# Reordering operand sums, stores and last transposes in an attention and mixture-of-experts kernel with nested Strassen products

## Chip, cores and metric

One core of one Trainium2 chip. The metric is device time in microseconds (us) of one execution; a kernel's figure is the median of its executions. "Span" is the length of the one execution that the profiler took; it is about 1.8 us shorter than the time of the same execution. "Half clock" is a stretch in which the trace shows TensorE's granted clock at one half; the "mean clock" of an execution is that clock's average over it, and 1.000 is full.

## The reference

Linear attention with decay over 4 batches, 8 heads, 768 positions and 64 channels, in blocks of 64, then a four-expert feed-forward on the 3072 x 512 result. All is fp32.

```python
# attention, per block b of 64 positions
intra = ((qb @ kb.T) * Dmask) @ vb
out   = intra + (qb * lam_pow) @ kv_state
kv_state = lam_block * kv_state + (kb * rev_pow).T @ vb
# bridge: x = out as (3072, 512)
p = domain_probs / (domain_probs.sum(-1, keepdims=True) + 1e-09)
for e in range(4):                       # w1: 512 x 1024, w2: 1024 x 512
    h = np.maximum(x @ w1[e], 0.0)
    out += p[:, e:e + 1] * (h @ w2[e])
```

## The kernel before

The expert layers are three groups of 1024 tokens times four experts: twelve **units**. Each x @ w1 of a unit is done by two levels of a seven-product scheme (products M1 to M7, each made of seven inner products), so most matmuls take *sums* of blocks as operands. VectorE and GpSimd make those sums; VectorE also takes the products out of PSUM ("evacuation", `m<-pg`, `m<-pM`) and adds them up (`hS`). Unit one runs beside the attention. From unit two on, TensorE interleaves the second layer of a unit with the first layer of the next. In the last group the second layer is nested too, and its sums (`T1` to `T4`, tiles `hT`) are made on the way.

Python decides the order at build time with lists of closures: `chores` is GpSimd's work and its loads, handed out by `pump` as time slots `now[0]` go by; `queue` holds stores; `background` and `aside` are put-off VectorE and GpSimd steps that `rest()` and `take()` draw from between products. The places that matter here:

```python
def own_x(m):                             # unit two's x operands, (...) is a cut
    ...
            for n, x, y, op in T_OPS:     # four 128x256 subtractions, tile "ops"
                b[n] = s[:, SLOT[n]]
                tt(nc.vector, b[n], b[x], b[y], op)
    ...
def own_w1(m):                            # unit two's w1 operands
    ...
        tt(nc.gpsimd, b[n], b[x], b[y], op)
    ...
def own(m):
    fed[0, 1, m] = own_x(m), own_w1(m)

# the list of GpSimd's work while unit one's last direct products run
chores.extend((*prepare_w2(1), *raws, pause(4), mine["M1"], sum_own("S1", "A21", "A22", ALU.add)))

# last group: operand sums on VectorE, block by block
for at in BLOCKS:
    for n in names:                       # ("T1", "T3", "T2") or ("T4",)
        ...                               # ScalarE copies one block to PSUM, VectorE subtracts
        work.append([lambda n=n, at=at: total(n, at)])
```

## Time and profile before

| kernel before | value |
|---|---|
| time, median of 3 | 1205.98 us (1205.05 to 1207.86) |
| span profiled | 1202.6 us |
| TensorE busy | 1188.0 us, 99% |
| waits of TensorE for unit two's first operands, then for the last unit, then at the end, by spacing | 3.03; 2.02 + 1.23 + 0.72; 0.77 + 0.77 us |
| half clock after the first of these | 3.413 us long, 1.76 us lost |

"By spacing" means: the distance between the starts of two matmul records, less the 0.216 us that a 128x256 record takes when nothing is in the way (0.109 us for the 128x128 transposes at the end). It counts a little more than the idle time that the profile prints. With TensorE at 99%, only such places can be won; the prediction below shows the lines.

```profile
90.50 3.45 POOL L95 TENSOR_TENSOR w1o<-w1o,w1b 128x512 f32<-128x512 f32 x2
103.94 1.41 POOL L95 TENSOR_TENSOR ops<-w1o 128x256 f32<-128x256 f32 x2 [10.00 <-PE pg L733]
```

### The profile page before, as it was taken

How to read it: one execution, taken by the hardware profiler on the slowest of the kernel's cores; microseconds unless marked ns; L12 is line 12 of the kernel's file. 1: busy time of each engine (PE TensorE's matmuls, PEld its weight loads, DVE VectorE, ACT ScalarE, POOL GpSimd, SP SyncE). 2: the span in 40 equal slices, each digit the busy share in tenths (PEclk: the TensorE clock that was granted, in tenths of full speed). 3: DMA queues.
4: the chain of work that ended last, by engine and by line, in shares of the span. 5: the costliest groups of instructions: out<-in, count | busy, mean ns of one | idle time of the engine just before them, and what ended most of it. 6: DMA issues, size and time to landing. Idle time of an engine off the chain costs nothing.

```text
span 1202.6 us, 17908 instructions
## 1 busy us (share of the span) xinstructions
PE 1188.0 (99%) x6623; PEld 1031.2 (86%) x6623; DVE 793.2 (66%) x1318; ACT 261.9 (22%) x476; POOL 635.3 (53%) x600
## 2 busy tenths in 40 slices
PE   9999999999999999999999999999999999999988
PEld 8887888888888888888888888888888888888877
DVE  6597796477467656746755774764665667777774
ACT  3321122112112201311220120120133341241232
POOL 1874267355468800044425745416675774874873
PEclk9999999999999999999999999999999999999999
DMA  9874869999989985789987999898987566566542
GB/s 224 231 262 166 276 208 352 352 315 332 377 286 328 339 286 173 224 286 275 283 286 233 304 311 319 278 315 304 301 280 262 215 229 248 218 241 227 208 151 71
DMA packets 227447, 317.94 MB, mean 264 GB/s; under 512 B 91648, under 2 KB 168864, under 8 KB 227360
## 3 DMA queue, kind: packets, MB, share of 16 engines
q1 hardware_dynamic: 219920, 314.63, 77.6%
q10 hardware_dynamic: 7440, 2.17, 0.8%
q8 instruction: 52, 0.85, 0.3%
q14 instruction: 35, 0.29, 0.1%
HBM read 231.40 MB, written 85.34 MB: 263 GB/s over the span
## 4 chain that ended last, share of the span: by engine, by line
PE 90%; DVE 3%; SPq 3%; DMA 2%; POOL 1%; issue 1%; ACT 0%; DVEq 0%; POOLq 0%
PE pg L733 38%; PE q L787 33%; PE pq L958 12%; DVE m L95 2%; SPq L122 2%; PE sp L484 1%; PE op L512 1%; POOL w2o L95 1%; PE op L507 1%; PE qp L461 1%; PE kp L461 1%; PE pM L928 1%; DMA probs<-in_moe_domain_probs_dram 1%; DMA w1b<-in_moe_w_dram 1%; PE op L520 1%
## 5 line engine op out<-in xcount | busy, mean ns | idle before, releaser
L733 PE MATMUL pg<-xs_in,ws_in 128*128 128x256 f32 x1960 | 470.3, 380 | 0.7 <-DVE m L95 0.5
L733 PEld LDWEIGHTS pg<-xs_in,ws_in 128*128 128x128 f32 x1960 | 370.5, 190 | 53.9 <-DVE m L95 2.5
L95 DVE TENSOR_TENSOR m<-pg,m 128x512 f32<-128x512 f32 x451 | 307.7, 687 | 111.7 <-PE pg L733 101.5
L787 PE MATMUL q<-w2t,hS 128*128 128x256 f32 x1024 | 243.3, 380 | 0.0
L787 PEld LDWEIGHTS q<-w2t,hS 128*128 128x128 f32 x1024 | 192.9, 190 | 26.8 <-issue 0.3
L803 DVE SCALAR_TENSOR_TENSOR acc<-q,gate,acc 128x256 f32<-128x256 f32 x192 | 92.4, 481 | 174.0 <-PE q L787 173.1
L787 PE MATMUL q<-w2t,m 128*128 128x256 f32 x768 | 183.9, 383 | 0.0
L787 PEld LDWEIGHTS q<-w2t,m 128*128 128x128 f32 x768 | 145.9, 191 | 20.6 <-issue 0.2
L745 ACT ACTIVATE m<-m 128x512 f32<-128x512 f32 x132 | 83.0, 630 | 337.1 <-DVE m L95 335.3
L95 POOL TENSOR_TENSOR m<-m,xT 128x512 f32<-128x512 f32 x64 | 81.6, 1290 | 78.4 <-ACT m L745 46.3
L95 POOL TENSOR_TENSOR kn<-kn,s_decay 128x512 f32<-128x512 f32 x20 | 22.1, 1105 | 170.4 <-PE kp L461 130.3
L95 DVE TENSOR_TENSOR sums<-pq,sums 128x256 f32<-128x256 f32 x154 | 64.1, 421 | 49.3 <-PE pq L958 41.7
L958 PE MATMUL pq<-acc,w2t 128*128 128x256 f32 x352 | 86.7, 379 | 1.9 <-POOL acc L95 1.9
L741 ACT COPY m<-pg 128x512 f32<-128x512 f32 x88 | 51.4, 585 | 154.6 <-PE pg L733 147.9
L95 DVE TENSOR_TENSOR m<-m,m 128x512 f32<-128x512 f32 x96 | 81.0, 847 | 0.0
L95 POOL TENSOR_TENSOR ops<-w2b 128x256 f32<-128x256 f32 x24 | 18.9, 807 | 109.6 <-DMA w2b<-in_moe_w_dram 109.6
L958 PEld LDWEIGHTS pq<-acc,w2t 128*128 128x128 f32 x352 | 66.8, 190 | 11.3 <-issue 2.2
L680 ACT ACTIVATE m<-m 128x512 f32<-128x512 f32 x48 | 30.3, 631 | 154.0 <-DVE m L95 154.0
L95 DVE TENSOR_TENSOR hS<-m,m 128x512 f32<-128x512 f32 x64 | 54.8, 861 | 8.4 <-ACT m L745 8.4
L95 POOL TENSOR_TENSOR acc<-hT,hT 128x512 f32<-128x512 f32 x32 | 40.1, 1270 | 32.5 <-DVE hT L95 19.5
L95 POOL TENSOR_TENSOR w2o<-w2b 128x512 f32<-128x512 f32 x32 | 41.8, 1326 | 24.2 <-DMA w2b<-in_moe_w_dram 21.4
L95 POOL TENSOR_TENSOR acc<-hT,acc 128x512 f32<-128x512 f32 x32 | 40.7, 1271 | 5.0 <-PE pq L958 2.7
(129 smaller groups left out, 1325.5 us busy)
## 6 DMA issues: line engine op xcount, KB each, us to landing
xs_in<-x_ops SPq DMA_DIRECT2D x70, 896.0 KB, 6.0
ws_in<-w_ops SPq DMA_DIRECT2D x70, 896.0 KB, 8.6
w2t<-w_ops SPq DMA_DIRECT2D x66, 256.0 KB, 6.6
w2t<-w_sums SPq DMA_DIRECT2D x64, 256.0 KB, 3.8
w_ops<-ops SPq DMA_DIRECT2D x28, 512.0 KB, 5.4
w2t<-in_moe_w_dram SPq DMA_DIRECT2D x48, 256.0 KB, 3.3
x_ops<-ops SPq DMA_DIRECT2D x17, 512.0 KB, 6.8
w2b<-in_moe_w_dram SPq DMA_DIRECT2D x32, 256.0 KB, 5.7
```

Source lines behind the costliest of these rows:

```text
L95: eng.tensor_tensor(out=o, in0=a, in1=b, op=op)
L122: nc.sync.dma_start(out=to[:, :, r], in_=of[:, :, r])
L461: nc.tensor.transpose(out=x[:, ac * C:(ac + 1) * C], in_=y[:, 2 * ac:2 * ac + 2].rearrange("p r d -> p (r d)"), identity=ident[:],)
L484: nc.tensor.matmul(out=sp[r][:, ac * C:(ac + 1) * C], lhsT=hc(kT)[half[r], ac], rhs=hc(qT)[half[r], ac], start=True, stop=True,)
L507: nc.tensor.matmul(out=op[r][half[x], a * C:(a + 1) * C], lhsT=kv[half[r], 2 * a + x], rhs=hc(qs)[half[r], 2 * a + x], start=(a == 0), sto ...
L680: nc.scalar.activation(out=o[:], in_=o[:], func=AF.Relu)
L733: nc.tensor.matmul(out=p[:, j * 256:(j + 1) * 256], lhsT=ws[i][:, j * P:(j + 1) * P], rhs=xs[i], start=(fresh and j == 0), stop=True, skip ...
L741: nc.scalar.copy(out=new[at][:], in_=p[:])
L745: nc.scalar.activation(out=new[at][:], in_=new[at][:], func=AF.Relu)
L787: nc.tensor.matmul(out=p[:, s * DH:(s + 1) * DH], lhsT=h[A_OF[m]][:, c * 256 + s * P:c * 256 + (s + 1) * P], rhs=fed2[g, e, m][uu][:, c], ...
L803: nc.vector.scalar_tensor_tensor(out=o, in0=x, scalar=w, in1=o, op0=ALU.mult, op1=ALU.add)
L958: nc.tensor.matmul(out=p[:, 0:256], lhsT=fed3[e, m, x // 2][:, x % 2, c * P:(c + 1) * P], rhs=b[B_OF[i]][:, c * 256:(c + 1) * 256], start= ...
```

## The change

Its intent is to take away TensorE's remaining waits: (1) at the start, half of the first q and k loads are issued from another engine; (2) for unit two, the w1 operands of the first product are made ahead of w2's sums, and its x operands come earlier in VectorE's order; the stores of x operands wait eight slots in a queue of their own, `late`; (3) for the last unit, VectorE makes T1's four sums first, a put-off step is skipped at the unit's first slot, and M3's GpSimd sums are made in the unit before; (4) at the end, the last blocks are transposed and stored in pieces. Cut to its core:

```diff
-                    nc.sync.dma_start(out=to[:, :, r], in_=of[:, :, r])
+                    by = nc.scalar if n < 2 and r == 1 else nc.sync
+                    by.dma_start(out=to[:, :, r], in_=of[:, :, r])
 (...)
+        while late and (force or late[0][0] <= now[0]):
+            late.pop(0)[1]()
 (...)
-        for at in BLOCKS:
-            for n in names:
+        for part in names:
+            for at in BLOCKS:
+                for n in part:
 (...)   # names: (("T1",), ("T3", "T2")), (("T4",),)
-        keep_own(("x", 0, m), x_ops[0, MS.index(m)], pieces)
+        late.append((now[0] + 8, keep_own(("x", 0, m), x_ops[0, MS.index(m)], pieces)))
 (...)
-    chores.extend((*prepare_w2(1), *raws, pause(4), mine["M1"], sum_own("S1", "A21", "A22", ALU.add)))
+    w2_steps = prepare_w2(1)
+    chores.extend((
+        lambda: own_weights("M1"), sum_own("S1", "A21", "A22", ALU.add), *w2_steps[0:4], mine["M1"], *w2_steps[4:],
+        raw["A12"],
+    ))
 (...)
-                inner_sums(ahead[1], SEQ3[0])
+                inner_sums(ahead[1], SEQ3[0], nested)
+                if ahead[1] == EARLY[0]:
+                    inner_sums(*EARLY, True)
 (...)
-                elif ahead or x % 2 == 0:
+                elif ahead or x % 2 == 0 and x + i:
                     rest()
 (...)
-    give("M4", 1, ("s1",))
+    give("M4", 0, ("q01",), (0,))
+    give("M4", 1, ("q11",), (0,))
```

Cut: small tiles in place of stage tiles for two w1 blocks, a faster pace of handing out GpSimd's work, early operand steps put first in line in `chores`, the order of some loads, and, with the new order of the T sums, an earlier release: the first five of them are put off by four slots in place of six.

More of the change, by code (lines that the diff above doesn't have):

```diff
@@ L121, in load @@
                 for r in range(2):
-                    nc.sync.dma_start(out=to[:, :, r], in_=of[:, :, r])
+                    by = nc.scalar if n < 2 and r == 1 else nc.sync
+                    by.dma_start(out=to[:, :, r], in_=of[:, :, r])
             nat[n, name] = x[:].rearrange("p (h d) -> p h d", d=D)
-    lam_bc = consts.tile([P, H], FP32, name="lam_bc")
-    nc.scalar.dma_start(out=lam_bc[:], in_=lam.partition_broadcast(P))
     w1_ops = dram.tile([E, 7, P, 7, 256], FP32, name="w1_ops")
@@ L135 @@
     X_AT = {n: i for i, n in enumerate(("M1", "M7", "M6", "M4", "M5", "M2", "M3"))}
-    chores, queue, results, made = [], [], [], set()
+    chores, queue, late, results, made = [], [], [], [], set()
     LEFT = 1
@@ L333, in raw_w1 @@
         i, j = int(name[1]) - 1, int(name[2]) - 1
-        if name == "A22":
+        if name in ("A21", "A22"):
             to = tuple(small("w1b")[:] for _ in range(2))
@@ L344, in sum_w1 @@
     def sum_w1(e, name, a, b, op):
-        if e == 0:
+        if e == 0 or name == "S1":
             to = tuple(small("w1o")[:] for _ in range(2))
@@ L352, in sum_w1 @@
         w1_now[e][name] = to
+    lam_bc = consts.tile([P, H], FP32, name="lam_bc")
+    nc.scalar.dma_start(out=lam_bc[:], in_=lam.partition_broadcast(P))
     for n, names in ((0, "qk"), (1, "qk"), (0, "v"), (2, "qk"), (1, "v"), (3, "qk")):
@@ L440, in take @@
         for x, f in enumerate(queue):
-            if force or getattr(f, "at", 0) <= now[0]:
+            if force or getattr(f, "at", 0) <= now[0] and getattr(f, "can", lambda: True)():
                 queue.pop(x)()
@@ L554, in end @@
                 if n == g * CPG + CPG // 2 - 1:
-                    chores.extend(early)
+                    chores[0:0] = early
                 if n == g * CPG + CPG - 1:
@@ L617, in total, with inner_sums @@
             outer[e][name][at] = o
-        work = []
-        for at in BLOCKS:
-            for n in names:
-                a, _ = of[n]
-                k = len(work)
-                if n in ("T1", "T3", "T4"):
-                    x = lambda a=a, at=at, tag={"T1": "s0", "T3": "s1", "T4": "s" + "01"[k % 2]}[n]: bring(a, at, tag)
-                    if not work:
-                        work.append([x])
-                    else:
-                        work[-1].append(x)
-                work.append([lambda n=n, at=at: total(n, at)])
-        background.extend(after(6, lambda fs=fs: [f() for f in fs]) for fs in work)
-    def inner_sums(e, m):
+        work, tags = [[]], itertools.cycle(("s0", "s1"))
+        for part in names:
+            for at in BLOCKS:
+                for n in part:
+                    if n != "T2":
+                        work[-1].append(lambda a=of[n][0], at=at, tag=next(tags): bring(a, at, tag))
+                    work.append([lambda n=n, at=at: total(n, at)])
+        background.extend(after(4 + 2 * (i > 4), lambda fs=fs: [f() for f in fs]) for i, fs in enumerate(work))
+    EARLY = E - 1, "M3"
+    def inner_sums(e, m, behind=False):
+        if (e, m) in within:
+            return
         blk, b = outer[e][B_OF[m]], {}
@@ L642, in total @@
                 b.update({"B" + at: blk[at] for at in BLOCKS})
-            b[name] = opool.tile([P, W], FP32, name="acc")
+            b[name] = small("h" + name) if (e, m) == EARLY else opool.tile([P, W], FP32, name="acc")
             tt(nc.gpsimd, b[name][:], b[x][:], b[y][:], ALU.subtract)
-        aside[0:0] = [lambda n=n, x=x, y=y: total(n, x, y) for n, x, y, _ in T_OPS]
+        work = [after(0, lambda n=n, x=x, y=y: total(n, x, y)) for n, x, y, _ in T_OPS]
+        for f in work:
+            f.can = lambda: len(blk) == 4
+        if behind:
+            aside.extend(work)
+        else:
+            aside[0:0] = work
     SEQ = ("M1", "M5", "M6", "M2", "M7", "M3", "M4")
@@ L690, in keep @@
             if g == LAST:
-                outer_sums(e, *{(0, 1): ("T1", "T3", "T2"), (1, 0): ("T4",)}.get((i, j), ()))
+                outer_sums(e, *{(0, 1): (("T1",), ("T3", "T2")), (1, 0): (("T4",),)}.get((i, j), ()))
                 return
@@ L898, with give @@
     RESULT = {"M2": (0, 0), "M3": (0, 1), "M4": (1, 0), "M5": (1, 1)}
-    def give(m, t, tags):
+    def give(m, t, tags, dds=(0, 1)):
         joined(m)
@@ L904, in give @@
         p, o = bank(tags[t % len(tags)], "yp"), small("y")
-        for dd in range(2):
+        w = len(dds) * P
+        for x, dd in enumerate(dds):
             for s in range(2):
                 nc.tensor.transpose(
-                    out=p[:, s * DH + dd * P:s * DH + (dd + 1) * P], in_=sums[m][:, 2 * dd + t, s * P:(s + 1) * P],
+                    out=p[:, s * w + x * P:s * w + (x + 1) * P], in_=sums[m][:, 2 * dd + t, s * P:(s + 1) * P],
                     identity=ident[:],
                 )
-        nc.scalar.copy(out=o[:], in_=p[:])
-        r = LAST * G + j * W + t * 256
+        nc.scalar.copy(out=o[:, 0:2 * w], in_=p[:, 0:2 * w])
+        r, d = LAST * G + j * W + t * 256, i * DH + dds[0] * P
         nc.sync.dma_start(
-            out=out[r:r + 256, i * DH:(i + 1) * DH].rearrange("(s p) d -> p s d", p=P),
-            in_=o[:].rearrange("p (s d) -> p s d", s=2),
+            out=out[r:r + 256, d:d + w].rearrange("(s p) d -> p s d", p=P),
+            in_=o[:, 0:2 * w].rearrange("p (s d) -> p s d", s=2),
         )
@@ L1018, in own_w1, with own_weights @@
             tt(nc.gpsimd, b[n], b[x], b[y], op)
-        keep_own(("w1", 1, m), w1_ops[1, MS.index(m)], (
+        store(keep_own(("w1", 1, m), w1_ops[1, MS.index(m)], (
             ((0, 1), c[0][:, 0:256].unsqueeze(1)), ((1, 5), s[:]), ((5, 7), c[1].rearrange("p (a f) -> p a f", a=2)),
-        ))
+        )))
         return {i: b[A_OF[i]] for i in A_OF}
     def keep_own(what, to, pieces):
-        store(lambda: ([nc.sync.dma_start(out=to[:, x:y], in_=of) for (x, y), of in pieces], made.add(what)))
+        return lambda: ([nc.sync.dma_start(out=to[:, x:y], in_=of) for (x, y), of in pieces], made.add(what))
+    own_ops = {}
+    def own_weights(m):
+        own_ops[m] = own_w1(m)
     def own(m):
-        fed[0, 1, m] = own_x(m), own_w1(m)
+        if m not in own_ops:
+            own_weights(m)
+        fed[0, 1, m] = own_x(m), own_ops[m]
     def direct_product(e, m, blocks, tags):
@@ L1074 @@
     blocks = {}
+    raw = {n: lambda n=n: raw_w1(1, n) for n in ("A11", "A12", "A21", "A22")}
     m1, m2 = (direct_product(0, m, blocks, ("g1", "g3")) for m in ("M1", "M2"))
@@ L1096 @@
             sum_w1(0, "S4", "A12", "S2", ALU.subtract)
-            chores.extend(prepare_w2(0))
+            chores.extend((*prepare_w2(0), *(raw[n] for n in ("A11", "A22", "A21"))))
         more = list(between.get(i, ()))
@@ L1134, in sum_own @@
         return lambda: sum_w1(1, name, a, b, op)
-    raws = [lambda n=n: raw_w1(1, n) for n in ("A11", "A12", "A21", "A22")]
-    chores.extend((*prepare_w2(1), *raws, pause(4), mine["M1"], sum_own("S1", "A21", "A22", ALU.add)))
+    w2_steps = prepare_w2(1)
[3 more added lines that the diff above has]
+    ))
     for m in SEQ0[2:]:
@@ L1147 @@
                 now[0] += 1
-                pump()
+                pump(0.75)
     start, w1_steps = now[0], prepare_w1(2)
@@ L1161 @@
         pause_till(1, 4), mine["M2"], sum_own("S4", "A12", "S2"),
-        pause_till(2, 4), mine["M7"], *w1_steps[0:2],
-        pause_till(3, 4), mine["M3"], *w1_steps[2:4],
-        pause_till(4, 4), mine["M4"], *w1_steps[4:],
+        pause_till(2, 4), mine["M7"],
+        pause_till(3, 4), mine["M3"], *w1_steps[0:2],
+        pause_till(4, 4), mine["M4"], *w1_steps[2:],
     ))
     fill3 = [(e, m, k) for e in range(E) for m in SEQ3 for k in range(4)]
-    after_last = {"M2": (None,) * 5 + (("M3", 0), ("M3", 1)), "M4": (("M5", 0), ("M5", 1), ("M2", 0), ("M2", 1), ("M4", 0))}
+    after_last = {
+        "M2": (None,) * 5 + (("M3", 0), ("M3", 1)),
+        "M4": (("M5", 0), ("M5", 1), ("M2", 0), ("M2", 1), ("M4", 0, (1,)), ("M4", 1, (1,))),
+    }
     steps = attention(1)
@@ L1228 @@
                     if y:
-                        give(*y, ("s0", "s1"))
+                        give(*y[:2], ("s0", "s1"), *y[2:])
                 if x == 0 and at * 7 + i >= 6 and fill:
@@ L1236 @@
                 pump(PACE[g])
-    give("M4", 1, ("s1",))
+    give("M4", 0, ("q01",), (0,))
+    give("M4", 1, ("q11",), (0,))
     pump(force=True)
-    assert not (background or aside or chores or queue or results)
+    assert not (background or aside or chores or queue or late or results)
 _INS = ['q', 'k', 'v', 'lam', 'moe_domain_probs', 'moe_w1', 'moe_w2']
```

## The prediction

> **What bounds the kernel now.** I read the page's first two parts, then the waits of TensorE, then the order of time on TensorE and VectorE around each wait.
>
> ```profile
> PE 1188.0 (99%) x6623; PEld 1031.2 (86%) x6623; DVE 793.2 (66%) x1318; ACT 261.9 (22%) x476; POOL 635.3 (53%) x600
> PE   9999999999999999999999999999999999999988
> ```
>
> TensorE is busy from end to end, and the order of instructions says that the change keeps every matmul: the same 3,424 matmul instructions in both kernels, with two groups of transposes regrouped at the end. So it can win only what TensorE loses to waiting or to a slow clock. The trace records matmuls 0.216 us apart when nothing is in the way (eight 128x256 records in 1.73 us). Where do they come later? Two views name the places: the waits of TensorE, and the stretches with their mean clock.
>
> ```profile
> PE pg L733 <- DVE ops L95: 2.9, 1, 2.9
> PE pq L958 <- POOL acc L95: 1.9, 1, 1.9
> PE yp L907 <- DVE sums L95: 1.2, 2, 0.6
> PE pq L958 <- DVE sums L95: 1.1, 1, 1.1
> PE pg L958 <- DVE sums L95: 0.6, 1, 0.6
> PE kp L461 <- DMA kn<-in_k_dram: 0.5, 1, 0.5
> ```
> ```profile
> 80.00:100.00 20.00, 17.13 (x73) 14.44 (x72) 18.04 (x29) 8.44 (x14) 11.13 (x8) 0.91 0.46 149
> ```
>
> In the second fence the columns after the 20.00 are busy time of the five engines, then the granted clock: 0.91, where the neighbouring stretches have 1.00. The order of time on TensorE shows both losses.
>
> ```profile
> 91.08 1.03 PE L733 MATMUL pg<-xT,w1b 128*128 128x256 f32 x4
> 94.98 1.40 PE L733 MATMUL pg<-ops 128*128 128x256 f32 x4 [2.87 <-DVE ops L95]
> 96.17 3.32 PE L787 MATMUL q<-w2t,m 128*128 128x256 f32 x8
> 99.33 1.03 PE L733 MATMUL pg<-ops 128*128 128x256 f32 x4
> ```
>
> Four matmuls from 91.08 should be followed at 91.95 and are followed at 94.98: 3.03 us. The next twelve take 99.33 - 94.98 = 4.35 us instead of 12 x 0.216 = 2.59: 1.76 us more, at half clock. This one wait costs 4.8 us. What it waits for is VectorE's subtractions for unit two's x operands, queued behind other sums:
>
> ```profile
> 91.67 1.15 DVE L95 TENSOR_TENSOR hS<-m,m 128x512 f32<-128x512 f32 x1
> 92.86 1.63 DVE L95 TENSOR_TENSOR hS<-hS,m 128x512 f32<-128x512 f32 x1
> 94.42 0.75 DVE L95 TENSOR_TENSOR ops<-xT 128x256 f32<-128x256 f32 x2
> ```
>
> VectorE is not waiting there; it is busy for 39.76 of the 40 us from 57 to 97 (stretch view), so it is a local bound.
>
> [...] the same hS sum lasts 0.67 us at best and up to 1.75 while GpSimd works. [...] The trace shows an issue of a q half at 0.43 to 0.51 us on the sync queue, and its landings 0.44 us apart from 3.94 us on: already about as slow as the transfers.
>
> **The change part by part.**
>
> *Start.* Half of the first two chunks' q and k loads (four of eight) moves to the scalar queue. In the first 20 us the warm-up matmuls cover the loads: the first transposes start at 5.48 us straight after them. What could gain is the DMA stream that ends in the waits at 21 to 22.6 us (0.39 + 0.64 us late, by spacing). The DMA share is 0.58 from 2 to 3 us and over 1.0 after, so only about 0.3 us of stream can be brought forward: **0.3 us**.
>
> *Unit two's first operands.* In VectorE's order the four `ops` subtractions move from behind four evacuations and five sums to just behind the first evacuation and one sum of the last direct product. Counting from the evacuation that started at 87.47 us, at 0.60 us for each 128x512 step and 0.40 for each 128x256: evacuation, one sum, four subtractions end near 90.3 us, before the 91.95 at which TensorE asks. The 4.8 us wait goes. But VectorE's work isn't less, only reordered, and TensorE will then run 4.8 us earlier into it. VectorE idled 1.85 + 0.71 us between 97.67 and 101.33 in the old kernel, waiting for TensorE; with these filled, its evacuation that ended at 102.0 ends about 99.45. TensorE needs it for the matmul that stood at 103.64, thus at 98.84: 0.6 us late. Then the four `xt` subtractions of the next operand stand ahead of the next evacuation (before they were behind it): 0.60 + 4 x 0.40 + 0.40 + 0.60 + 0.60 from 99.45 gives 103.3, and TensorE, whose matmul was at 106.23, wants it at 101.4. So about 1.9 us come back as smaller waits, and no half clock should follow such short ones. Net **2.9 us**. GpSimd's part: w1's operands go ahead of w2's sums and are ready by about 61 us (its last w2 sum of unit one ends at 54.95, the loads need some 4 us, four steps 3.6); those w2 sums are wanted only after 200 us. The x stores delayed by eight slots are wanted again a full unit later, so they cost nothing.
>
> *Last unit.* Three waits, by spacing 2.02, 1.23 and 0.72 us, at 1147.6, 1156 and 1163 us.
>
> ```profile
> 1148.52 0.69 DVE L95 TENSOR_TENSOR hT<-hp,m 128x512 f32<-128x512 f32 x1 [0.58 <-ACT hp L611]
> 1149.13 0.74 DVE L95 TENSOR_TENSOR sums<-pq,sums 128x256 f32<-128x256 f32 x2
> 1149.65 2.83 PE L958 MATMUL pq<-acc,w2t 128*128 128x256 f32 x12 [1.85 <-POOL acc L95]
> ```
>
> The page names GpSimd for the first, but the operand sums of that product had ended by 1136.5. What ends just before 1149.65 is VectorE's first `sums` evacuation, begun at 1149.13 behind three hT sums that waited for gates and copies. The second wait is of the same kind: three hT sums in a row at 1154.65 to 1156.4. In the new order, T1's four sums come first, mostly ahead of the last unit's evacuations, and then one hT per pair of evacuations. A pair of products takes TensorE 1.73 us; two evacuations and one hT take 2 x 0.34 + 0.60 or a little over, which fits. I leave 0.4 of the first wait and 0.15 of the second. The third follows the join's copy to PSUM, whose place is unchanged, so it stays. Also M3's operand sums (four x 1.27 us on GpSimd) go ahead of the last gates and are ready near 1147 instead of 1152.3. Net 1.6 + 1.1 = **2.7 us**.
>
> *End.* The half of M4's blocks that is ready is turned before the last product. That takes away the wait before it (0.77 us by spacing). After the last product two half copies (0.37 us each, the size that the xT copies show, against 0.59) and two issues (0.37 each) stand where one full copy and issue stood; these overlap, so the last landing comes 0 to 0.2 us sooner. **0.9 us.**
>
> Sum 0.3 + 2.9 + 2.7 + 0.9 = 6.8 us; 1205.98 - 6.8 = 1199.2, which I round to **1199**.
>
> **The rivals.** (a) *VectorE remains the bound of 57 to 97 us.* GpSimd will work there almost without the pauses it had (5.2, 3.9 and 2.8 us, waiting for loads), and each overlap can stretch a VectorE sum by up to 1 us. If it loses 2 to 3 us more, the operands are ready late, and the gain of that part falls to 0 to 1: 1201.5 to 1202. For it: the 39.76 of 40 us. Against: GpSimd's work is the same amount, and the old waits hid 2.2 us of slack before 91.95.
> (b) *The whole 4.8 us is gained,* because the slow sums at 91.67 and 92.86 (1.5 us over their best) no longer meet GpSimd, which is through earlier. Then TensorE finds its evacuations in time: about 1197.
> (c) *A new wait in the sync queue or a stage buffer:* operands wait longer for their late stores, and loads stand in order behind them; a load that then lands late stops TensorE between 100 and 300 us, with the half clock again if the gap nears 3 us. Against: the old trace has no TensorE wait over 0.3 us on that stretch, and w2 tiles landed 10 us before use. It would make 1203 to 1206.
> (d) *Nothing at the last unit,* if the GpSimd label is the true cause and M3's sums merely displace the gates: 1201.5.
>
> **Range and chances.** All candidates add to at most 1.0 + 4.8 + 4.0 + 1.7 = 11.5 us, 1.0% of the time, so a 2% change (24 us) is out of reach, and nothing in the change adds matmuls. Between (b) with a good end and (a) with (d): 1196 to 1203. Faster by over 2%: 0.01, same 0.98, slower 0.01.
>
> **What would show it.** Right: TensorE's waits list loses the 2.9 us of `DVE ops`, and the stretch 80 to 100 us has clock 1.00; between 92 and 105 us there are waits for `m` evacuations of 0.5 to 2 us in all; the 1.9 and 1.1 us waits of the last unit shrink below 0.5 each, and the one near 0.6 stays; one `yp` wait is left. Wrong: a `DVE ops` wait and a clock under 1.00 still there; a DMA as releaser of TensorE between 60 and 300 us; or a last unit whose waits keep their sum. A time below 1196 would mean that VectorE's backlog didn't matter; above 1203, that a new wait took the old one's place.

## The result, and the profile after

| | before | changed |
|---|---|---|
| time, median of 4 | 1205.51 us (1203.98 to 1207.86) | 1198.28 us (1197.33 to 1199.55) |
| ratio | 1 | 0.9939 [0.9920, 0.9958] |
| span profiled | 1202.6 us | 1197.8 us |

A ratio here and below is the mean time of one kernel's fast runs over that of the other's of the same rounds, so not quite the ratio of the medians; in brackets is its 95% interval. The difference of 7 us is real, and smaller than 2%. All outputs are right.

The busy times of the changed kernel hardly move, as expected of a reordering:

```profile
PE 1187.6 (99%) x6623; PEld 1031.3 (86%) x6623; DVE 792.1 (66%) x1318; ACT 261.5 (22%) x478; POOL 636.1 (53%) x600
```

TensorE's waits in the changed kernel (engine, tile and line that waited, releaser, then total us, times, longest us). The 1.9 and 1.1 us of the last unit are gone. In the first row the wait of 2.9 for `ops` has become one of 1.7 for an evacuation `m`.

```profile
PE pg L740 <- DVE m L95: 2.2, 3, 1.7
PE pg L966 <- DVE sums L95: 0.6, 1, 0.6
PE yp L915 <- DVE sums L95: 0.5, 1, 0.5
PE pq L966 <- POOL m L95: 0.5, 1, 0.5
```

The stretch from 80 to 100 us (busy time of TensorE, its weight loads, VectorE, ScalarE and GpSimd, then clock, DMA share and GB/s) still has clock 0.91. GpSimd is now busy for 17.56 of the 20 us, against 11.13 before. The order of time on TensorE, VectorE and GpSimd in the changed kernel shows what happened:

```profile
80.00:100.00 20.00, 18.34 (x76) 15.22 (x75) 19.90 (x26) 8.41 (x14) 17.56 (x14) 0.91 0.41 151
```
```profile
91.83 1.03 PE L740 MATMUL pg<-xT,w1b 128*128 128x256 f32 x4
94.51 1.10 PE L740 MATMUL pg<-ops 128*128 128x256 f32 x4 [1.66 <-DVE m L95]
95.62 3.68 PE L794 MATMUL q<-w2t,m 128*128 128x256 f32 x8
```
```profile
89.15 1.81 DVE L95 TENSOR_TENSOR ops<-xT 128x256 f32<-128x256 f32 x2
90.99 2.78 DVE L95 TENSOR_TENSOR ops<-xT,ops 128x256 f32<-128x256 f32 x2
93.69 0.68 DVE L95 TENSOR_TENSOR m<-pM,m 128x512 f32<-128x512 f32 x1
```
```profile
86.42 2.19 POOL L95 TENSOR_TENSOR ops<-w1o 128x256 f32<-128x256 f32 x2
88.69 1.12 POOL L95 TENSOR_TENSOR ops<-ops,w1o 128x256 f32<-128x256 f32 x1
89.88 0.79 POOL L95 TENSOR_TENSOR ops<-w1o,ops 128x256 f32<-128x256 f32 x1
90.63 2.85 POOL L95 TENSOR_TENSOR w1o<-w1o,w1b 128x512 f32<-128x512 f32 x2
```

VectorE's four subtractions did move forward, by 5.3 us. But they took 1.81 + 2.78 = 4.6 us, not 1.6, because they now lie beside GpSimd's work (86.42 to 98 us without a pause). Record by record, each of the four ends 0.28 or 0.29 us after one of GpSimd's sums does (90.09 after 89.81, 90.95 after 90.67, 92.36 after 92.08, 93.77 after 93.48). The evacuation behind them came at 93.69, and TensorE stood still for 1.66 us in front of it; then the clock dropped to one half (eight records took 3.68 us, where e1's took 1.99).

At the last unit and at the end, in TensorE's order of the changed kernel, what is left is 0.67 + 0.74 us by spacing, and one wait of 0.68 at the end:

```profile
1147.23 2.83 PE L966 MATMUL pq<-acc,w2t 128*128 128x256 f32 x12 [0.51 <-POOL m L95]
1160.29 2.83 PE L966 MATMUL pg<-acc,w2s 128*128 128x256 f32 x12 [0.58 <-DVE sums L95]
1191.60 0.60 PE L915 MATMUL yp<-ident,sums 128*128 128x128 f32 x4
1193.58 0.66 PE L915 MATMUL yp<-ident,sums 128*128 128x128 f32 x4 [0.52 <-DVE sums L95]
```

The kernel before had two waits among these transposes:

```profile
1196.03 0.63 PE L907 MATMUL yp<-ident,sums 128*128 128x128 f32 x4 [0.61 <-DVE sums L95]
1198.13 0.63 PE L907 MATMUL yp<-ident,sums 128*128 128x128 f32 x4 [0.61 <-DVE sums L95]
```

### The profile page after: what moved, and what is told of

The parts are those of the page before. It is cut to its first block, busy times and chain, and to the rows that moved or that the text cites.

```text
span 1197.8 us, 17886 instructions
## 1 busy us (share of the span) xinstructions
PE 1187.6 (99%) x6623; PEld 1031.3 (86%) x6623; DVE 792.1 (66%) x1318; ACT 261.5 (22%) x478; POOL 636.1 (53%) x600
## 4 chain that ended last, share of the span: by engine, by line
PE 92%; DVE 3%; DMA 2%; POOL 1%; SPq 1%; issue 1%; ACT 0%; ACTq 0%; DVEq 0%; POOLq 0%
PE pg L740 38%; PE q L794 33%; PE pq L966 12%; DVE m L95 2%; PE op L514 2%; PE sp L486 2%; PE pM L1058 1%; PE op L509 1%; PE kp L463 1%; SPq L123 1%; PE op L522 1%; PE qp L463 1%; DMA w2b<-in_moe_w_dram 1%; PE pM L936 1%; POOL m L95 1%
## 5 line engine op out<-in xcount | busy, mean ns | idle before, releaser
L95 POOL TENSOR_TENSOR w1o<-w1b 128x512 f32<-128x512 f32 x20 | 29.7, 1506 | 29.6 <-PE pg L740 15.0
```

Source lines behind the costliest of these rows:

```text
L95: eng.tensor_tensor(out=o, in0=a, in1=b, op=op)
```

## The experiments

Twelve kernels ran, in three sets of four; each set shares one chip and eleven executions of the kernel before. As single us are at stake and totals turn out to scatter by more, the table also gives, for each profiled execution, the parts of its trace: the start of unit two's first group of matmuls, the waits there by spacing (those over 0.25 us), whether a half clock followed, and the waits of the last unit and the end.

| kernel | median us (range) | ratio to before | group starts | waits 91 to 106 us | half clock there | last unit | end |
|---|---|---|---|---|---|---|---|
| before | 1205.51 | 1 | 91.08 | 3.03 | yes | 2.02 + 1.23 + 0.72 | 0.77 + 0.77 |
| e9 before again | 1203.28 (1200.19 to 1207.36) | 0.9988 [0.9971, 1.0005] | 92.46 | 3.46 | yes | 2.02 + 1.24 + 0.72 | 0.77 + 0.77 |
| changed | 1198.28 | 0.9939 [0.9920, 0.9958] | 91.83 | 1.82 | yes | 0.67 + 0.74 | 0.68 |
| e1 changed again | 1197.72 (1197.17 to 1198.53) | 0.9946 [0.9925, 0.9967] | 91.08 | 0.84 + 0.60 + 0.71 | no | 0.67 + 0.74 | 0.68 |
| e2 without start | 1198.41 (1196.74 to 1199.30) | 0.9951 [0.9931, 0.9970] | 90.87 | 1.47 + 0.60 + 0.71 | no | 0.67 + 0.74 | 0.68 |
| e3 last part alone | 1198.00 (1196.99 to 1201.16) | 0.9954 [0.9933, 0.9975] | 90.92 | 2.53 | no | 0.67 + 0.74 | 0.68 |
| e4 middle alone | 1202.79 (1201.79 to 1206.51) | 0.9991 [0.9969, 1.0012] | 92.29 | 0.96 + 0.60 + 0.71 | no | 2.01 + 1.23 + 0.72 | 0.77 + 0.77 |
| e8 end alone | 1201.57 (1199.42 to 1202.53) | 0.9980 [0.9963, 0.9997] | 90.49 | 3.13 | no | 2.02 + 1.23 + 0.72 | 0.68 |
| e6 x sums on GpSimd | 1195.63 (1195.15 to 1196.57) | 0.9932 [0.9917, 0.9948] | 90.65 | 0.80 | no | 0.67 + 0.74 | 0.68 |
| e7 GpSimd held | 1201.42 (1199.80 to 1201.66) | 0.9978 [0.9962, 0.9993] | 93.40 | 1.00 + 1.97 | no | 0.67 + 0.74 | 0.68 |
| e11 no late queue | 1196.58 (1195.78 to 1197.12) | 0.9929 [0.9917, 0.9941] | 90.87 | 1.32 | no | 0.67 + 0.74 | 0.68 |
| e12 old T order | 1200.86 (1200.55 to 1201.55) | 0.9966 [0.9953, 0.9978] | 90.69 | 0.99 + 0.60 + 0.72 | no | 0.74 + 0.92 + 1.61, half clock | 0.68 |

### Parts of the change alone (e1 to e4, e8)

e1 is the changed kernel itself. e2 is the changed kernel with all first loads on the sync queue (and, not shown, the decay load first again):

```diff
-                    by = nc.scalar if n < 2 and r == 1 else nc.sync
-                    by.dma_start(out=to[:, :, r], in_=of[:, :, r])
+                    nc.sync.dma_start(out=to[:, :, r], in_=of[:, :, r])
```

e3 is the kernel before with parts (3) and (4) only, e4 the kernel before with part (2) only, e8 the kernel before with part (4) only.

> The changed kernel again, as the common measure for the other runs. 0.994 of the kernel before, some 7 us less. If the half clock after the first wait of unit two comes in some executions only, the runs' mean clocks differ (1.000 against 0.998) and their spans by about 1.5 us; if it comes always, all clocks are near 0.999 or below.

> The changed kernel with all q and k loads on the sync queue again and the decay load first. Theory (the split delays the loads: the trace of the change has waits of 0.80 and 0.44 us by spacing at 21 and 22.5 us where before had 0.39 and 0.64, and the first group of unit two starts 0.75 us later): 0.3 to 0.8 us faster than the change. Rival (as predicted, the split brings 0.3 us): 0.3 us slower.

> The kernel before with only the parts for the last unit: operand sums across units, order of the outer sums, the last blocks in pieces. Theory: the three waits of the last unit fall from 3.97 to about 1.4 us by spacing and the end by 0.8, so 3.3 us less than before, 0.9973 of it; the wait for the DVE ops at 92 us stays as before. Rival (the last unit gains nothing without the earlier parts): within 0.5 us of before.

> The kernel before with only the parts for unit two: w1's operands ahead of w2's sums, x stores in the late queue, the early operand steps first in line. Theory: the 3.0 us wait shrinks to 1.8 or less, and with it 1.2 to 1.9 us are gained when the half clock still follows, 3 to 4 when it doesn't; over several runs 2 to 4 us less than before. Rival (the wait is only moved and the loads' start matters more): within 0.7 us of before.

> The kernel before, with only the turning of the last blocks in pieces. By my prediction's step for the end it gains 0.9 us (1204.5 where before gives 1205.4; 0.9993), and then the rest of what the last part did alone, 5.5 us of mean time, belongs to the operand sums of the last unit or to chance in the runs of before. Rival (the last part's gain over the 3.3 us that the traces show lies at the end): 2 us or more (0.998).

*The changed kernel again* (e1): 0.9946, as expected. None of its six executions has a mean clock below 0.999. Its waits at unit two, and one matmul without a wait, in TensorE's order:

```profile
92.79 1.10 PE L740 MATMUL pg<-ops 128*128 128x256 f32 x4 [0.68 <-DVE m L95]
96.32 1.10 PE L740 MATMUL pg<-ops 128*128 128x256 f32 x4 [0.43 <-POOL ops L95]
100.71 1.03 PE L740 MATMUL pg<-xT,w1b 128*128 128x256 f32 x4
104.01 1.10 PE L740 MATMUL pg<-xT,ops 128*128 128x256 f32 x4 [0.55 <-DVE m L95]
```

*The start* (e2): 1198.41 against 1197.72 us for e1, so 0.7 slower without the split, with intervals that overlap almost wholly, while its first group came at 90.87 against 91.08 us, 0.2 earlier. Neither a gain nor a loss from the split loads is shown; its theory isn't borne out.

*The last part* (e3): -5.5 us of mean time (1 - 0.9954 of 1205), more than the 3.3 us or so that the traces of before and changed had led me to expect. Its own trace gives less. From the first wait of the last unit to the end of the span, the kernel before takes 1202.6 - 1147.41 = 55.2 us, e8 1198.7 - 1144.71 = 54.0, e3 1196.1 - 1144.67 = 51.4. So the end is worth **1.2 us** and the last unit **2.6 us**, 3.8 in all. The same reading of e9 gives 55.2 again: these sections repeat to 0.1 us (with one exception, e4, whose end is that of before and took 55.0), while totals of one kernel scatter over 7 us. e8's 2.4 us of mean time, like e3's 5.5, therefore hold something that isn't in the parts that were changed (by chance, none of e8's six executions has a mean clock below 0.999, where five of the eleven of before in its set do), and the rival of e8 (2 us or more at the end) isn't supported by its trace.

*The middle* (e4): -1.1 us of mean time, with an interval that includes 0. The kernel before, run against itself (e9), gives as much (0.9988), so no gain is shown by totals. Its waits are 2.27 us, where before, e9 and e8 have 3.03 to 3.46, and e3 2.53. The stretch from unit two's first group to the first wait of the last unit says the same. Without a half clock it takes 1054.2 us in e8 and 1053.8 in e3, which lack this part, and 1053.2 to 1054.3 in e1, e2, e4 and e12, which have it: 0.2 us less on average. With a half clock it takes 1056.3 in before and 1056.2 in e9, and 1054.5 in the changed kernel: 1.6 to 1.8 less, from one trace. And e3, of the same set as e1 and without start and middle, is only 0.3 us slower than e1 by medians.

### The spread of the kernel before (e5, e9, e10)

In each set, the eleven executions of before lie between 1200 and 1208 us; e1's six lie within 1.4 us. My guess was the half clock that the trace of before shows behind the wait at 92 to 95 us. Filler matmuls that nobody reads were put into that wait:

```diff
+            if (g, e, m, i) == (0, 1, "M1", INNER[1]):
+                idle = bank("s0", "idle")
+                for _ in range(10):
+                    nc.tensor.matmul(out=idle[:, 0:256], lhsT=ident[:], rhs=xs["M1"], start=True, stop=True)
```

> The kernel before, with ten matmuls of 256 columns (0.216 us each, so about 2.2 us; their result is read by nobody) put ahead of the second inner product of unit two, in the 2.87 us for which TensorE stood still there at 94.98 us. No operand comes earlier, so by the waits alone the time is the same as before (1.000). Theory: the executions of the kernel before fall apart into about 1201 and about 1206 us because in some of them the idle stretch is followed by matmuls at half clock; without the idle stretch the mean clock of 80 to 100 us in the trace is 1.00, no execution is above 1203.5 us, and the mean is 2 to 3 us below before (0.998). Rival: the spread comes from elsewhere (the waits of the last unit, the transfers); then the executions spread over 1200 to 1207 us as those of before do, ratio 1.000.

> The kernel before, unchanged, built under another name: six more executions and one more trace of it. Theory (two things vary between executions of one kernel: the position of the first group of unit two, 90.5 to 93.9 us in the ten traces so far, set by the waits for loads in the first 25 us; and a half clock of 3.4 us after the wait for unit two's operands, in about half of the executions): the executions with a mean clock of 0.998 or less average about 3 us more than those with 0.999 or 1.000, the trace shows a wait of 2.8 to 3.2 us ahead of the second inner product, and a half clock after it only if this execution's mean clock is 0.998 or less. Rival (the spread has nothing to do with the clock): no such order by mean clock.

> The kernel with the ten unread matmuls a second time, because its first trace had the first group of unit two 2.8 us later than that of before, ahead of the place where the two kernels differ. Theory (that start was chance of one loading of the kernel, and the filled gap does away with the half clock): with a first group at 90.5 to 91.8 us the mean is 1202.0 to 1203.0, that of the executions of before that show no half clock, and no mean clock is below 0.999. Rival (the filler itself costs what it saves): 1204 to 1207 again, with the first group near 91 us.

By its total, the theory fell at first: e5 gave 1206.08 us (1204.34 to 1206.76), ratio 1.0015 [0.9997, 1.0033]; e10, the same kernel, 1203.83 (1203.38 to 1206.71), 0.9994 [0.9981, 1.0006]. The trace of e10 tells two reasons. The filler was mis-sized: its ten fp32 matmuls left *twenty* records (x20 below), so they took 20 x 0.216 = 4.3 us, about 1.3 longer than the wait that they were to fill; e10's mean of 1204.4 us is what its rival said (the filler costs what it saves):

```profile
91.43 1.03 PE L737 MATMUL pg<-xT,w1b 128*128 128x256 f32 x4
92.29 4.48 PE L732 MATMUL idle<-xT,ident 128*128 128x256 f32 x20
96.61 1.03 PE L737 MATMUL pg<-ops 128*128 128x256 f32 x4
```

And e5's first group started at 93.92 us, with nothing different in the kernel ahead of it: its waits for the first q and k loads (0.71 + 0.92 + 1.28 + 0.92 us between 7 and 24 us by spacing) were longer than those of before (0.39 + 0.64). Over the fourteen traces, this start lies anywhere from 90.5 to 93.9 us, whatever the kernel, and as widely among the five whose code up to there is that of before (before, e5, e8, e9, e10). Most of this spread is time for which TensorE stood idle before it (span up to the start, less TensorE's busy time): 1.4 us in e11 (start 90.87), 1.8 in before (91.08), 2.4 in e8 (90.49), 3.7 in e9 (92.46), 4.6 in e7 (93.40) and 5.1 in e5 (93.92), where 3.2 of them were waits for q and k loads. Why the same loads come later in one execution than in another wasn't found.

The clock itself did what the theory said. In e10 the stretch has clock 1.00, and none of the filler's eleven executions has a mean clock below 0.999. Of 39 executions of the kernel before (33 in the three sets, 6 in e9), the 22 with a mean clock of 0.998 or less average 1205.6 us, the 17 with 0.999 or more 1202.4. (The figure is rounded and only a hint: the changed kernel's first trace has a half clock at a mean of 0.999.) e9's own trace was of the first kind, with its half clock behind a gap of 3.29 us; e8 is of the second kind, although its gap was 2.97 us:

```profile
80.00:100.00 20.00, 16.54 (x69) 13.98 (x69) 19.38 (x30) 8.44 (x14) 10.89 (x8) 0.91 0.30 88
```
```profile
80.00:100.00 20.00, 17.03 (x80) 14.70 (x79) 19.02 (x30) 9.03 (x15) 10.90 (x8) 1.00 0.44 143
```

Why does the same gap slow the clock in one execution and not in the other? This is what the traces show. In all four that have a half clock inside the kernel, it starts a whole number of steps of 3.413 us (the length of the half clock itself in before, from 95.65 to 99.06 us) after the moment at which the clock first became full: 26 steps in before, 27 in e9, 26 in the changed kernel, 338 in e12. The step ahead of it held 2.74, 2.77, 1.66 and 1.86 us of TensorE's idle time. In e8 a step, counted in the same way, ended in the middle of the gap, which left 1.22 us in one and 1.75 in the next, and the clock stayed full. Where the steps fall differs from execution to execution (the clock first became full at 3.9 to 7.0 us). My reading of these few traces is therefore that a gap of 3 us is a lottery ticket: 1.76 us more, as after the 2.87 us of before, or nothing, as after the 2.97 of e8. Idle time in a step alone doesn't decide it: four steps with 1.85 us, at the last unit, stayed without a half clock, and one with 1.66 us, in the changed kernel, was followed by one. What does decide it was not shown.

So shortening a wait can also be worth the half clocks that no longer follow it: in e10's trace, with the gap filled, none did. For before that is an estimate of about 22/39 x 1.76 = 1.0 us on average, if each execution of the slower kind has one. It doesn't explain the whole 3.2 us between the two kinds; the rest stays open.

### What holds up unit two (e6, e7, e11)

Theory: the four subtractions are slow because GpSimd works beside them. e6 moves them to GpSimd itself, into its pause of 6.8 us; e7 lets GpSimd stand still until they are done; e11 puts the x stores back into the usual queue.

```diff
# e6
-                tt(nc.vector, b[n], b[x], b[y], op)
+                tt(nc.gpsimd if m == "M1" else nc.vector, b[n], b[x], b[y], op)
# e7: a 128x2 operation on GpSimd that reads the last of the four
-        mine["M5"], sum_own("S2", "S1", "A11"),
+        hold, mine["M5"], sum_own("S2", "S1", "A11"),
# e11
-        late.append((now[0] + 8, keep_own(("x", 0, m), x_ops[0, MS.index(m)], pieces)))
+        store(keep_own(("x", 0, m), x_ops[0, MS.index(m)], pieces))
```

> The changed kernel, with the four 128x256 subtractions that make the x operands of unit two's first product moved from VectorE to GpSimd, ahead of its w1 operands, where GpSimd stood still for 6.8 us. Theory (these four steps, 4.6 us long on VectorE beside GpSimd's w1 operands, are what TensorE waits for): the waits at 91 to 99 us fall from 2.1 us to below 0.5 us, the half clock there is gone, and the kernel is 1.5 to 3 us faster than the changed one (1195 to 1196.5 us; 0.992 to 0.993 of before). Rival (VectorE's backlog of evacuations is what counts, and GpSimd's overlap stretches them wherever the four steps are): the wait stays within 0.7 us of 2.1 us, time that of the changed kernel (0.9946).

> The changed kernel, with one tiny GpSimd operation ahead of the w1 operands of the product M5 that reads the last of the four x operands, so that GpSimd stands still until VectorE has made them. Theory (the four VectorE steps take 4.6 us only because GpSimd works beside them): they take 1.6 to 2.0 us, the wait of 0.7 to 1.8 us ahead of the second inner product goes to 0 to 0.3 us, and the time is 0.7 to 1.5 us below that of the changed kernel. Rival one (the steps are slow by themselves, or from the DMA traffic): they still take over 4 us and nothing changes. Rival two: GpSimd is late afterwards with the w1 operands of M5, and a new wait released by GpSimd of over 0.5 us comes in at 100 to 115 us; the time is the same or up to 1 us worse.

> The changed kernel, with the stores of unit two's x operands back in the usual queue of stores, not eight slots later. My prediction gave the late queue nothing. Theory: the same time as the changed kernel within 0.7 us, the waits of TensorE between 91 and 130 us the same within 0.5 us. Rival (the stores stand in the sync queue ahead of loads until VectorE is done, and so hold up operands): a wait of TensorE or of GpSimd for a load between 95 and 140 us that the changed kernel doesn't have, and 1 to 3 us more.

*e7* settles why they were slow. With GpSimd still, its order and VectorE's read:

```profile
92.07 0.20 POOL L1175 TENSOR_TENSOR idle<-ops 128x2 f32<-128x2 f32 x1 [4.03 <-DVE ops L95]
```
```profile
90.33 0.75 DVE L95 TENSOR_TENSOR ops<-xT 128x256 f32<-128x256 f32 x2
91.11 0.88 DVE L95 TENSOR_TENSOR ops<-xT,ops 128x256 f32<-128x256 f32 x2
```

0.75 + 0.88 = 1.63 us, as in the kernel before, against 4.6 in the changed one; and the wait ahead of the second inner product is gone. But the time is 3.7 us above e1's, not 0.7 to 1.5 below it as the theory said: GpSimd's 4 us come later, stretch VectorE's sums there (up to 1.75 us for a 128x512 sum that takes 0.68 undisturbed), and two new waits of 1.00 and 1.97 us stand at 101 and 105 us. That was the second rival, except that the trace names VectorE, not GpSimd, as the releaser. (Of the 3.7 us by which e7 is slower than e1, 2.3 lie in the chance of its start, 93.40 against 91.08.)

*e6* takes the four steps off VectorE, and the waits at 91 to 99 us vanish; 0.80 us at 101 us is left. In TensorE's order:

```profile
90.65 1.03 PE L740 MATMUL pg<-xT,w1b 128*128 128x256 f32 x4
91.51 1.03 PE L740 MATMUL pg<-ops 128*128 128x256 f32 x4
101.81 1.13 PE L740 MATMUL pg<-xT,ops 128*128 128x256 f32 x4 [0.64 <-DVE m L95]
```

The time, 1195.63 us, is the lowest of all twelve and inside what the theory expected; its rival (no change) fell. Each of its six executions is below every execution of the changed kernel, though of another set, and the intervals of the two ratios overlap. The traces speak for a real gain: from unit two's first group to the first wait of the last unit, e6 takes 1051.4 us and e1 1053.9.

*e11* surprised me. I had given the late queue nothing, and a rival said that without it the time would be worse. It was 1196.58 us, below all of the changed kernel's executions too, though of another set; the stretch up to the last unit takes 1052.9 us, 0.9 less than in e1. GpSimd and VectorE in e11:

```profile
100.12 2.93 POOL L95 TENSOR_TENSOR w1o<-w1o,w1b 128x512 f32<-128x512 f32 x2 [11.56 <-DMA w_sums<-w2o]
```
```profile
87.90 1.28 DVE L95 TENSOR_TENSOR ops<-xT 128x256 f32<-128x256 f32 x2
89.21 0.89 DVE L95 TENSOR_TENSOR ops<-xT,ops 128x256 f32<-128x256 f32 x2
```

GpSimd did wait for a store, as the rival said, for 11.56 us. But it was not needed in that time, and while it stood still VectorE's subtractions took 2.2 us. The same effect as in e7, by accident, and without the debt: only one wait of 1.32 us came back.

### What gained at the last unit (e12)

The changed kernel with the T sums in the old order, block by block. The edit (cut) also puts back what belongs to that order in the kernel before: all sums are put off by six slots, where the changed kernel puts off the first five by four, and the copies go to PSUM buffers in another turn. So e12 tests the order and the slots together. Everything else is as changed.

```diff
-        for part in names:
-            for at in BLOCKS:
-                for n in part:
+        for at in BLOCKS:
+            for n in names:
```

> The changed kernel, with the last unit's operand sums T1 to T4 on VectorE in the order of before (all sums of one block, then the next), but with M3's sums on GpSimd still made early. Theory (the order on VectorE makes the waits, the releaser GpSimd that the trace names is not the cause): the first two waits of the last unit come back, 1.2 to 2.0 us and 0.8 to 1.2 us by spacing against 0.67 and 0 in the changed kernel, the third stays at 0.7; 1.5 to 2.5 us slower than the changed kernel. Rival (GpSimd's early M3 sums are what helped): waits as in the changed kernel, 0.67, 0, 0.74, and the same time.

It is 3.1 us slower than e1 by medians (2.4 by the ratios, as the two belong to different sets), but not in the way that I had said. The first wait did *not* come back (0.74 us). In VectorE's order only one hT sum stands between the last `m<-pg` and the first `sums`, as in the changed kernel, where before had two and a wait for a copy between them:

```profile
1143.13 0.68 DVE L95 TENSOR_TENSOR m<-pg,m 128x512 f32<-128x512 f32 x1
1143.72 0.68 DVE L95 TENSOR_TENSOR hT<-hp,hT 128x512 f32<-128x512 f32 x1
1144.32 0.75 DVE L95 TENSOR_TENSOR sums<-pq,sums 128x256 f32<-128x256 f32 x2
```

So by elimination the first wait's gain belongs not to the order of T but to another part of (3). The put-off step that is skipped at the unit's first slot fits these lines; it wasn't tried alone, and neither were M3's early sums, which are the rival of e12's expectation. What gained there stays open. The order of T, with its slots, matters later. GpSimd now waited 7.70 us for hT and was late with the sums behind it, and TensorE waited twice for GpSimd, with a half clock after:

```profile
1155.89 2.50 POOL L95 TENSOR_TENSOR acc<-hT,hT 128x512 f32<-128x512 f32 x2 [7.70 <-DVE hT L95]
```
```profile
1157.22 1.13 PE L971 MATMUL pg<-acc,w2s 128*128 128x256 f32 x4 [0.76 <-POOL acc L95]
1159.79 4.55 PE L971 MATMUL pg<-acc,w2s 128*128 128x256 f32 x12 [1.44 <-POOL acc L95]
```

T1 first, or its earlier release, is what lets GpSimd begin early (at 1150.61 in the changed kernel). The label GpSimd is true here. For the first wait of before it is false: there, as in the changed kernel and in e12, TensorE goes on 0.10 us after VectorE's first `sums` ends (1149.55 and 1149.65 in before).

## Why the prediction was right or wrong

The time (1199 predicted, 1198.3 measured) and the direction were right. The sum was right partly by luck.

- **The bound.** Right: the matmuls stayed, and everything won lies in waits and clock of TensorE.
- **Start, 0.3 us.** Not shown; e2 is within the scatter.
- **Unit two, net 2.9 us.** This step failed. The failed term is "0.40 for each 128x256": the four subtractions took 4.6 us, not 1.6. I had read 0.40 off lines in which GpSimd stood still (94.42 us, in its pause from 93.95 to 103.94), and moved them to where it works; my own rival (a) said that such overlaps stretch sums, and I weighed it by the amount of GpSimd's work, not by its place. "The 4.8 us wait goes" became: 3.03 us of waiting fell to 2.15 in e1, 2.77 in e2 and 1.82 in the changed kernel's first trace, and there the half clock of about 1.8 us followed all the same. By waits the part is worth 0.3 to 1.2 us, and by totals 1.1 (e4, interval including 0).
- **The debt, "1.9 us come back as smaller waits".** Half right: 0.60 + 0.71 us. The 0.71 in e1 stands where it was forecast, ahead of the matmul that stood at 106.23 (now 104.01), whose evacuation came behind four `xt` subtractions. The 0.60 stands elsewhere: the matmul that stood at 103.64 didn't wait (100.71), and the third inner product did (96.32); that its size is the forecast one is luck. The trace names GpSimd's `ops` as its releaser, but in e6 and e7 the same matmuls started (94.10 and 96.85) before GpSimd's same step was done (97.8 and 104.4). What else ended just before is ScalarE's copy `m<-pg`, at 96.18, behind an activation that began when VectorE's evacuation ended, at 95.04: the same backlog by a path that I didn't have, read from the trace and not tested. Also "no half clock should follow such short ones" (none follows the waits of 1.85 and 1.07 us at the last unit of before) was wrong once, after 1.66 us.
- **Last unit, 2.7 us.** Measured 2.6, and the third wait stayed at 0.74 as said. But the reason for the first wait was only half right: it did end with VectorE's `sums`, but e12 shows that the order of T1 to T4 isn't what took it away, and what did stays open. For the waits after it, order and slots together count.
- **End, 0.9 us.** Measured 1.2. One transpose wait went (0.77 + 0.77 us became 0.68), and the last pieces overlap a little better: from the last four transposes to the end of the span it takes 4.2 us, where before takes 4.5.
- **The x stores, "cost nothing".** Wrong in sign, if the totals of two sets may be compared: without the delay the kernel is 1.1 us faster by medians (e11).
- **What made the sum come out.** The sections give 2.6 + 1.2 us for the last unit and the end, and 0.2 to 1.8 for the middle. The mean fell by 7. About 1 us more is the estimate for half clocks that became rarer. The last 0.4 to 2 us are not accounted for; the start of unit two, which drifts over 3.4 us between traces, is large enough to hold them.

Rival (a), VectorE as the local bound stretched by GpSimd, came closest for the middle; (b) is what e6 nearly reached; (c) and (d) fell.

## What to carry to other kernels

A duration read off a trace belongs to its neighbourhood: the same four 128x256 fp32 subtractions on VectorE took 1.63 us with GpSimd idle (e7) and 4.6 us beside its sums (the changed kernel; GpSimd's 128x256 sums took 0.8 to 1.1 us there, its 128x512 ones 1.4). In before, the 128x512 `hS` sums, of two SBUF tiles, took 0.67 to 1.75 us, and the `m<-pg` evacuations of the same size, with one operand in PSUM, 0.67 to 0.69. So before moving a VectorE step with two SBUF operands, look at what GpSimd does at the place where it will land, and use the duration that such steps have there. If GpSimd has a pause nearby, giving it the step (e6) or leaving it idle at that time (e11) can be worth more than the reordering (2.5 and 0.9 us less than e1, from one trace each), while holding it back where its work is needed soon (e7) only moves the wait. And where single microseconds are at stake, compare sections of traces, from one landmark matmul to the next, as well as totals: here sections repeated to 0.1 us, in one case to 0.3, and totals of one kernel scattered over 7.
